# A decode step of attention and MLP on one core: eight neighbouring result rows, a second accumulator bank near the end, and re-cut weight loads

## The chip, the cores and the metric

The kernel runs on one core of a Trainium2 chip. The metric is device time in microseconds. Before the change three runs gave 212.78, 212.80 and 212.83 us, a median of 212.8. The core has these engines: TensorE (PE in the profile) multiplies matrices, VectorE (DVE) and ScalarE (ACT) do elementwise work, GpSimd (POOL) does a little at the start, and SyncE (SP) issues almost all transfers. Sixteen DMA engines move the data between device memory and the core's working memory (SBUF). Matmul results go to PSUM[...].

## What is computed

Four tokens (batch 4, one position each) of width 576 go through a layer that adds three terms:

```python
x = A_x                                    # [4, 1, 576]
xn = _layernorm(x)
out = x + A(xn) + B(xn)

# A: attention over a window of the cache
W = 2048                                   # the last 2048 of 8192 positions
q = xn @ wq                                # 32 heads of 128; 16 key/value heads
p = softmax((q . k_window) * 128 ** -0.5)
A = (p @ v_window) @ wo                    # wo: [4096, 576]

# B: an MLP; with one position the shifted first half of it gives zero
x1 = xn
B = x1 + gelu(layernorm(x1) @ w3) @ w4     # w3: [576, 4608], w4: [4608, 576]
```

In the reference B's first half pads and shifts along the sequence. With a sequence of one, every shifted part is zero, so w1 and w2 are not read. What has to be read is 87.17 MB: keys and values of the window (16 + 16 loads of 2 MB), wq and wo (4.7 MB each), w3 and w4 (5.3 MB each).

## The kernel before

The program's order is written out by hand, so that each engine executes its instructions in the order of the source. SyncE issues the loads in this order: wq, then K and V by head, with a quarter of wo ahead of every fourth V, w3 after the V of head 2, and w4 after the last V. K and V share six buffers, and a load is issued when a buffer comes free. Each load is one instruction for all 128 partitions; the transfers that one queue was given are done in order.

**Weight tiles.** D is 576 = 4 x 128 + 64. The first 512 rows of wq and of w3 are laid out with four neighbouring rows in one partition, so that one partition of the "main" part is 4 rows of wq in one run of 32 KB (w3: 36 KB). Before, this main part comes in two loads (lines 119 to 121 for wq, `load_w3` at 129 to 133), each with half of every partition's run. The last 64 rows come in a third load, spread over 128 partitions. `load_w4` brings w4's 36 row groups ("rows" below: each is 128 x 576) in pieces, cut at the points of `W4_PIECES`.

**The main loop** goes over the 16 key/value heads. For head t: VectorE transposes K (`k_transpose`), TensorE forms the scores (`k_scores`), the softmax of head t-1 and the value product (`pv`) of head t-2 run in the gaps, and the outputs of head t-3 are transposed and summed (`o_turn`, `o_sum`). After every fourth head `o_spread`, `o_pick` and `o_proj` bring the attention result into shape (the tile `op`) and multiply it with a quarter of wo. In the turn of head 7 the MLP's first product and gelu run (`mlp_g`, `mlp_turn`, `mlp_act`), whose result is the tile `gT`.

**The accumulator.** Everything that ends in the result is added up in one PSUM bank, `acc`: the layernormed x plus x (`idz`), the output projection, and the MLP's second product (`mlp_out`). The stationary operand has 32 columns, in which the four batch values stand in columns 0, 8, 16 and 24 (step `RS` = 8) with zeros between. `acc_matmuls` does two matmuls for each weight row: result columns 0 to 287 into partitions 0 to 31, columns 288 to 575 into partitions 32 to 63. So two neighbouring matmuls always stand in different groups of 32 partitions.

**The end.** After the loop come the last two heads, then w4's pieces in the order of arrival, with the last quarter of `o_proj` between the second and the third. Then VectorE casts 64 x 288 values (line 601), and SyncE stores the rows 0, 8, 16, ... of the 64 with a three-dimensional pattern (line 602).

Of the kernel before, what the change touches and what calls it, by code (L numbers as in the profile page):

```python
# [8 lines left out]
ACT = mybir.ActivationFunctionType  # L9
ALU = mybir.AluOpType  # L10
AX = mybir.AxisListType
BF16 = mybir.dt.bfloat16
F32 = mybir.dt.float32
# [9 lines left out]
def kernel(  # L23
# [14 lines left out]
    nc = tc.nc  # L38
    P = 128
    B, Sq, D = A_x.shape  # L40
# [4 lines left out]
    F = B_w3.shape[1]  # L45
    assert Sq == 1 and Dh == P and rep == 2 and B == 4 and D == 576
    KJ = 4
    NQ = Hq * Dh
    NF = F // P
    NFH = NF // 2  # L50
# [3 lines left out]
    QD = 32  # L54
# [3 lines left out]
    CW = D // 2  # L58
# [8 lines left out]
    o2 = out.flatten_outer_dims()  # L67
# [14 lines left out]
    const = ctx.enter_context(tc.tile_pool(name="const", bufs=1))  # L82
# [4 lines left out]
    ps_acc = ctx.enter_context(tc.tile_pool(name="ps_acc", bufs=1, space=PSUM))  # L87
# [3 lines left out]
    wo_tiles = {}  # L91
    kv_tiles = {}
    WOH = 8
    WOR = WOH
    WOD = P // WOH
    WOQ = WOH // rep
# [12 lines left out]
    def part(n, parts=P):  # L109
        lo = cut["at"]  # L110
        cut["at"] = lo + n
        assert cut["at"] <= WOR * D
        return first[0:parts, lo:lo + n]
# [2 lines left out]
    nc.scalar.dma_start(out=x_bf[:], in_=x2)  # L116
    wq_sb = wp.tile([P, KJ * NQ + NQ // 2], BF16, tag="w", name="wq_sb")
    wq_main = A_wq[0:KJ * P, :].rearrange("(p j) n -> p (j n)", j=KJ)
    for e in range(2):
        lo, hi = e * 2 * NQ, (e + 1) * 2 * NQ  # L120
        nc.sync.dma_start(out=wq_sb[:, lo:hi], in_=wq_main[:, lo:hi])
    nc.sync.dma_start(out=wq_sb[:, KJ * NQ:], in_=A_wq[KJ * P:D, :].rearrange("r (e f) -> (r e) f", e=2))

    def load_wo(p):
# [3 lines left out]

    def load_w3():
        t = wp.tile([P, KJ * F + F // 2], BF16, tag="w", name="w3_sb")  # L130
        src = B_w3[0:KJ * P, :].rearrange("(p j) f -> p (j f)", j=KJ)
        for e in range(2):
            nc.sync.dma_start(out=t[:, e * 2 * F:(e + 1) * 2 * F], in_=src[:, e * 2 * F:(e + 1) * 2 * F])
        nc.sync.dma_start(out=t[:, KJ * F:], in_=B_w3[KJ * P:D, :].rearrange("r (e f) -> (r e) f", e=2))
        w_tiles["w3"] = t

    W4_PIECES = [0, 10, NFH, NFH + 10, NFH + 14, NF]

    def load_w4():
        t = wp.tile([P, NF, D], BF16, tag="w", name="w4_sb")  # L140
        for lo, hi in zip(W4_PIECES, W4_PIECES[1:]):
            e = lo // NFH
# [8 lines left out]
    ident_f = ident_w[:, 0:P]  # L151
# [7 lines left out]
    def cleared(shape, name):  # L159
        t = const.tile(shape, BF16, name=name)  # L160
        flat = t[:] if len(shape) == 2 else t[:].rearrange("p a b -> p (a b)")
        flat = flat.bitcast(F32)
        nc.scalar.activation(out=flat, in_=zero[:].bitcast(F32).to_broadcast(list(flat.shape)), func=ACT.Copy)
        return t
# [2 lines left out]
    ln2T = cleared([P, KJ + 2, QD], "ln2T")  # L167
    ZP = (NSL - 1) * NJ
    qz = cleared([P, ZP + Hkv * 4 * P], "qz")
    gT = cleared([P, NF, QD], "gT")  # L170
    op = cleared([P, WOR, QD], "op")

    RS = QD // B
    acc = ps_acc.tile([P, CW], F32)
    nc.vector.memset(acc[:], 0.0)


    def layernorm(dst_f, dst_bf, src):
        st = small.tile([B, 2, nc.vector.BN_STATS_DIM], F32, tag="ln_st")
        nc.vector.bn_stats(out=st[:, 0, :], in_=src[:, 0:D // 2])  # L180
        nc.vector.bn_stats(out=st[:, 1, :], in_=src[:, D // 2:D])
        mv = small.tile([B, nc.vector.BN_AGGR_DIM], F32, tag="ln_mv")
        nc.vector.bn_aggr(out=mv[:], in_=st[:].rearrange("p a s -> p (a s)"))
        rstd = small.tile([B, 1], F32, tag="ln_rstd")
        nc.vector.tensor_scalar_add(out=rstd[:], in0=mv[:, 1:2], scalar1=eps)
        nc.gpsimd.tensor_tensor(out=rstd[:], in0=rstd[:], in1=neg_half[:], op=ALU.pow)
        nc.vector.tensor_scalar(out=dst_bf[:], in0=src[:], scalar1=mv[:, 0:1], scalar2=rstd[:, 0:1],
                                op0=ALU.subtract, op1=ALU.mult)
        if dst_f is not None:
            nc.vector.tensor_scalar(out=dst_f[:], in0=src[:], scalar1=mv[:, 0:1], scalar2=rstd[:, 0:1],  # L190
                                    op0=ALU.subtract, op1=ALU.mult)
# [28 lines left out]
    for kb in range(NQD):  # L220
        nc.vector.tensor_copy(out=sel[:, :, :, kb, :],
                              in_=ident_bf[:].rearrange("p (ib i e) -> p ib e i", ib=2, e=2))
# [19 lines left out]
    with nc.allow_low_precision("zeros and ones"):  # L242
# [7 lines left out]
                          in_=sel_j[:].unsqueeze(1).to_broadcast([P, NG, NJ]))  # L250
# [5 lines left out]
    own = const.tile([P, WOH], F32)  # L256
    nc.vector.reduce_sum(out=own[:], in_=ident_f[:].rearrange("p (h d) -> p h d", h=WOH), axis=AX.X)

    idz = const.tile([B, QD], F32)
    nc.gpsimd.memset(idz[:], 0.0)  # L260
    nc.gpsimd.tensor_copy(out=idz[:, 0:QD:RS], in_=ident_f[0:B, 0:B])
    xsum = xn_f
    nc.vector.tensor_tensor(out=xsum[:], in0=xn_f[:], in1=x_bf[:], op=ALU.add)
    for i in range(2):
        nc.tensor.matmul(out=acc[i * QD:(i + 1) * QD, :], lhsT=idz[:], rhs=xsum[:, i * CW:(i + 1) * CW],
                         start=False, stop=False, skip_group_check=True)
    ln2_bf = part(D, B)
    layernorm(None, ln2_bf, xn_bf)
    transposed(ln2_bf, ln2T)
# [24 lines left out]
    for r in range(2):  # L294
        nc.vector.tensor_copy(out=q_bf[:, r],
                              in_=qT_ps[:, r].rearrange("p u (g x) -> p g u x", g=NQD)[:, :, :, 0:B])
    qs_ps = ps_m.tile([P, Hkv, 4, rep, B], F32, tag="m", name="qs_ps")
    for ie in range(4):
        ib, e = divmod(ie, 2)
        nc.tensor.matmul(out=qs_ps[:, :, ie], lhsT=sel[:, ib, e].rearrange("p k i -> p (k i)"),  # L300
                         rhs=q_bf.rearrange("p r g u b -> p (r g u b)"), start=True, stop=True)
    for kb in range(NQD):
        rows = slice(kb * QD, (kb + 1) * QD)
        dst = qz[rows, ZP:].rearrange("p (x m) -> p x m", m=P)[:, :, kb * QD:kb * QD + NJ].rearrange("p x (b r) -> p x b r", r=rep)
        src = qs_ps[rows].rearrange("p h i r b -> p (h i) b r")
# [2 lines left out]
        else:  # L308
            nc.vector.tensor_copy(out=dst, in_=src)  # L309


    def acc_matmuls(lhsT, rhs):
        for i in range(2):
            nc.tensor.matmul(out=acc[i * QD:(i + 1) * QD, :], lhsT=lhsT, rhs=rhs[:, i * CW:(i + 1) * CW],  # L314
                             start=False, stop=False, skip_group_check=True)

    S_ps = {}
    E = {}
# [77 lines left out]
    def o_turn(h):  # L396
        oT = ps_m.tile([P, NSL, P], F32, tag="m", name="oT")
        o = O_sb.pop(h)
        for s in range(NSL):
            nc.tensor.transpose(out=oT[:, s, :], in_=o[:, s, :], identity=ident_w[:, s * NJ:s * NJ + P])  # L400
        st["oT", h] = oT

    def o_sum(h):
        oT = st.pop(("oT", h))
        v = oT[:].rearrange("p s (g x) -> p (s g) x", g=NQD)[:, :, 0:NJ].rearrange("p g (b r) -> p b r g", r=rep)
        k = h % WOQ
        if k == 0:
            st["on"] = small.tile([P, WOH, B], BF16, tag="on", name="on")
        with nc.allow_low_precision("summed in float32"):
            nc.vector.reduce_sum(out=st["on"][:, k * rep:(k + 1) * rep, :].rearrange("p r b -> p b r"),  # L410
                                 in_=v, axis=AX.X)
# [12 lines left out]
    def o_pick(h):  # L424
        if h % WOQ < WOQ - 1:
            return
        R = st.pop("R")
        mk = small.tile([P, WOR, WOH, B], BF16, tag="mk")
        nc.vector.tensor_tensor(out=mk[:], in0=R[:],
                                in1=own[:].unsqueeze(1).unsqueeze(3).to_broadcast([P, WOR, WOH, B]), op=ALU.mult)  # L430
        with nc.allow_low_precision("one term is not zero"):
            nc.vector.reduce_sum(out=op[:, :, 0:QD:RS], in_=mk[:].rearrange("p i h b -> p i b h"), axis=AX.X)

    def o_proj(h):
        if h % WOQ < WOQ - 1:
            return
        for i in range(WOR):
            acc_matmuls(op[:, i, :], wo_tiles[h // WOQ][:, i, :])

    G_CHUNKS = [(e, 4 * g, 4) for e in range(2) for g in range(NQD)] + [(e, 16, 2) for e in range(2)]  # L440
    xs = const.tile([P, NF, B], F32, name="g_x")
# [31 lines left out]
    def mlp_act():  # L473
        u = const.tile([P, NF, B], F32, name="g_u")
        nc.vector.tensor_tensor(out=u[:], in0=xs[:], in1=xs[:], op=ALU.mult)
        nc.vector.tensor_scalar(out=u[:], in0=u[:], scalar1=GELU_A, scalar2=1.0, op0=ALU.mult, op1=ALU.add)
        nc.vector.tensor_tensor(out=u[:], in0=u[:], in1=xs[:], op=ALU.mult)
        nc.scalar.activation(out=u[:], in_=u[:], func=ACT.Tanh, scale=GELU_C)
        nc.vector.tensor_scalar(out=u[:], in0=u[:], scalar1=0.5, scalar2=0.5, op0=ALU.mult, op1=ALU.add)
        nc.vector.tensor_tensor(out=gT[:, :, 0:QD:RS], in0=u[:], in1=xs[:], op=ALU.mult)  # L480

    def mlp_out(lo, hi):
        w4 = w_tiles["w4"]
        for i in range(lo, hi):
            acc_matmuls(gT[:, i, :], w4[:, i, :])


    order = [("K", 0), ("K", 1), ("K", 2)]
# [24 lines left out]
    for t in range(Hkv):  # L513
        hm, hv, hf, hp = t - 1, t - 2, t - 3, t - 4
        for s in range(NSL):
            if s == NSL - 1 and hm >= 0:
                sm_turn(hm)
            n = t * NSL + s + 1
# [68 lines left out]
    o_turn(hl - 1)  # L587
    o_sum(hl - 1)
    pieces = list(zip(W4_PIECES, W4_PIECES[1:]))
    mlp_out(*pieces[0])  # L590
    o_turn(hl)
    o_sum(hl)
# [1 line left out]
    o_pick(hl)  # L594
    mlp_out(*pieces[1])
    o_proj(hl)
    for lo, hi in pieces[2:]:
        mlp_out(lo, hi)

    fin = const.tile([2 * QD, CW], out.dtype)  # L600
    nc.vector.tensor_copy(out=fin[:], in_=acc[0:2 * QD, :])
    nc.sync.dma_start(out=o2.rearrange("b (i n) -> i b n", i=2), in_=fin[0:2 * QD:RS, :])


# [28 lines left out]
```

## Time and profile before

| | us |
|---|---|
| median of three runs | 212.8 |
| profiled execution, span | 211.0 |
| TensorE busy | 150.4 (71%) |
| VectorE busy | 121.3 (57%) |
| ScalarE busy | 33.9 (16%) |
| load queue (q1), packets' time as a share of 16 engines' span | 97.2% |
| HBM read | 87.17 MB, 413 GB/s over the span |

The span is measured from the first to the last instruction of one profiled execution; the run's time has 1.8 us more around it. The page shows busy time by engine, a line for the DMA engines in forty slices of the span, and a chain of work followed back from the last instruction. By line that chain puts 29% of the span on the loads of w3 and w4, 26% on V, and 12% on K; by engine 67% on DMA and 18% on TensorE. In the timeline a row gives start, length, engine, source line, operation, output and inputs, and how many instructions are merged; in brackets is the idle time ahead of it, and what ended it. SPq is SyncE's queue: the length there is the time of issuing, and the data comes later. For a group of merged matmuls the length is that of the whole group.

### The profile page before, as it was taken

The numbers are of one execution on the slowest core, as the hardware profiler recorded it, in microseconds if no ns is written. First come the engines' busy times: TensorE is split into PE (matmuls) and PEld (weight loads), VectorE is DVE, ScalarE is ACT, GpSimd is POOL, SyncE is SP. The second block draws the span as 40 slices with busy tenths as digits, with TensorE's granted clock in tenths as the row PEclk, the third lists the DMA queues.
The fourth block names the chain that finished last, engine by engine and source line by source line (L and its number), as shares of the span: only waits on it lengthen the run. The fifth ranks groups of instructions, "written<-read, shape, count | busy, mean of one in ns | idle before, by whom it ended". The sixth has DMA issues, their size and how long they took to land.

```text
span 211.0 us, 2402 instructions
## 1 busy us (share of the span) xinstructions
PE 150.4 (71%) x955; PEld 62.2 (29%) x955; DVE 121.3 (57%) x216; ACT 33.9 (16%) x63; POOL 2.8 (1%) x15
## 2 busy tenths in 40 slices
PE   0386695869395009669999499968693967898982
PEld 0122232224132003214454144334240322433561
DVE  4832989485731082825725968985867284763220
ACT  7703101021102000202121121120211020202300
POOL 4010000000000000000000000000000000000000
PEclk9999579799859655957999669999998596969998
DMA  7999999999999999999999999999999999999990
GB/s 246 435 413 441 422 441 410 443 435 413 450 419 426 438 419 429 434 444 432 416 438 435 416 427 437 435 432 424 436 426 426 420 444 435 422 429 429 425 382 30
DMA packets 6797, 87.32 MB, mean 414 GB/s; under 512 B 758, under 2 KB 770, under 8 KB 1282
## 3 DMA queue, kind: packets, MB, share of 16 engines
q1 hardware_dynamic: 6778, 87.17, 97.2%
q8 instruction: 7, 0.11, 0.2%
q14 instruction: 4, 0.03, 0.0%
q10 hardware_dynamic: 8, 0.00, 0.0%
HBM read 87.17 MB, written 0.00 MB: 413 GB/s over the span
## 4 chain that ended last, share of the span: by engine, by line
DMA 67%; PE 18%; DVE 7%; issue 4%; ACT 1%; SPq 1%; POOL 0%; POOLq 0%; DVEq 0%
DMA w_sb<-in_B_w_dram 29%; DMA vn<-in_A_v_cache_dram 26%; DMA kn<-in_A_k_cache_dram 12%; PE S L335 9%; DVE kt L215 3%; PE g_ps L453 2%; PE q_ps L277 2%; PE O L387 2%; PE oT L400 1%; PE acc L314 1%; DMA first<-in_A_x_dram 1%; DVE qz L309 1%; PE gT_ps L465 1%; DVE mx L341 1%; PE S L357 1%
## 5 line engine op out<-in xcount | busy, mean ns | idle before, releaser
L335 PE MATMUL S<-kt,qz 128*128 128x512 bf16 x256 | 82.0, 452 | 3.1 <-DVE kt L215 3.1
L215 DVE STREAM_TRANSPOSE kt<-kn 128x1024 int32<-128x1024 int32 x64 | 76.8, 1221 | 10.3 <-DMA kn<-in_A_k_cache_dram 9.4
L387 PE MATMUL O<-vn,PT 128*32 128x512 bf16 x256 | 27.8, 434 | 38.5 <-DMA vn<-in_A_v_cache_dram 36.9
L335 PEld LDWEIGHTS <-qz 128*128 128x128 bf16 x256 | 22.2, 106 | 43.2 <-issue 28.5
L363 ACT ACTIVATE E<-S 128x512 bf16<-128x512 f32 x16 | 9.5, 597 | 123.4 <-PE S L357 123.4
L387 PEld LDWEIGHTS <-PT 128*32 128x32 bf16 x256 | 7.3, 95 | 47.2 <-DVE kt L215 23.8
L369 DVE STREAM_TRANSPOSE PT<-E 128x512 bf16<-128x512 bf16 x16 | 11.4, 711 | 14.3 <-ACT E L363 14.3
L353 DVE TENSOR_REDUCE nm<-mg 8x1 bf16<-8x16 f32 x16 | 2.5, 154 | 20.3 <-PE mg L348 20.2
L394 ACT ACTIVATE O_sb<-O,rd 128x512 f32<-128x512 f32 x16 | 11.0, 687 | 16.5 <-issue 11.0
L410 DVE TENSOR_REDUCE on<-oT 128x8 bf16<-128x128 f32 x16 | 4.6, 286 | 15.7 <-PE oT L400 15.7
L400 PE MATMUL oT<-ident_w,O_sb 128*128 128x128 f32 x64 | 11.8, 315 | 0.0
L341 DVE TENSOR_REDUCE mx<-S 128x1 f32<-128x512 f32 x16 | 10.5, 658 | 1.3 <-PE S L335 1.3
L400 PEld LDWEIGHTS oT<-ident_w,O_sb 128*128 128x128 f32 x64 | 9.6, 167 | 5.4 <-issue 3.9
L357 PE MATMUL S<-nm,j_row 8*128 8x512 bf16 x16 | 6.9, 431 | 0.0
L373 PEld LDWEIGHTS dn<-rs,same_j 128*128 128x128 f32 x32 | 5.8, 188 | 2.9 <-ACT E L363 0.7
L326 PE MATMUL S<-negbig,ohT 4*128 4x512 bf16 x16 | 6.2, 385 | 0.0
L314 PE MATMUL acc<-w_sb,gT 128*32 128x288 bf16 x72 | 5.3, 287 | 1.2 <-DMA w_sb<-in_B_w_dram 1.2
L348 PE MATMUL mg<-dm,sel_jb 128*8 128x16 bf16 x16 | 2.8, 175 | 3.7 <-DVE dm L343 3.7
L348 PEld LDWEIGHTS <-sel_jb 128*8 128x8 bf16 x16 | 1.3, 83 | 12.6 <-issue 6.7
L453 PE MATMUL g_ps<-w_sb,ln2T 128*32 128x512 bf16 (+1 forms) x50 | 4.9, 443 | 0.0
L314 PE MATMUL acc<-wo_sb,op 128*32 128x288 bf16 x64 | 4.6, 287 | 0.0
L373 PE MATMUL dn<-rs,same_j 128*128 128x1 f32 x32 | 4.6, 212 | 0.0
(89 smaller groups left out, 72.8 us busy)
## 6 DMA issues: line engine op xcount, KB each, us to landing
kn<-in_A_k_cache_dram SPq DMA_DIRECT2D x16, 2048.0 KB, 22.3
vn<-in_A_v_cache_dram SPq DMA_DIRECT2D x16, 2048.0 KB, 23.9
wo_sb<-in_A_wo_dram SPq DMA_DIRECT2D x4, 1152.0 KB, 25.8
w_sb<-in_B_w_dram SPq DMA_DIRECT2D x2, 2304.0 KB, 31.4
wq_sb<-in_A_wq_dram SPq DMA_DIRECT2D x2, 2048.0 KB, 9.6
w_sb<-in_B_w_dram SPq DMA_DIRECT2D x2, 1440.0 KB, 29.2
w_sb<-in_B_w_dram SPq DMA_DIRECT2D x3, 576.0 KB, 30.5
w_sb<-in_B_w_dram SPq DMA_DIRECT2D x1, 1152.0 KB, 28.7
```

Source lines behind the costliest of these rows:

```text
L215: nc.vector.transpose(out=kt[:], in_=src)
L314: nc.tensor.matmul(out=acc[i * QD:(i + 1) * QD, :], lhsT=lhsT, rhs=rhs[:, i * CW:(i + 1) * CW], start=False, stop=False, skip_group_check= ...
L335: nc.tensor.matmul(out=S_ps[h][:], lhsT=qz[:, z0:z0 + P], rhs=kt[:, ib, :, e:2 * QD:2].rearrange("p c k -> p (c k)"), start=False, stop=Fa ...
L341: nc.vector.reduce_max(out=mx[:], in_=S_ps[h][:], axis=AX.X)
L357: nc.tensor.matmul(out=S_ps[h][:], lhsT=j_row[:], rhs=st.pop(("nm", h))[:, 0:1].to_broadcast([NJ, NW]), start=False, stop=False, skip_grou ...
L363: nc.scalar.activation(out=E[h][:].rearrange("p c k -> p (c k)"), in_=S_ps.pop(h)[:], func=ACT.Exp, scale=scale, accum_out=rs[:])
L369: nc.vector.transpose(out=PT[h][:], in_=E.pop(h)[:])
L373: nc.tensor.matmul(out=dn[:], lhsT=same_j[:], rhs=st.pop(("rs", h))[:], start=True, stop=True)
L387: nc.tensor.matmul(out=O_ps[h][g * QD:(g + 1) * QD], lhsT=PT[h][:, c, :], rhs=vn[:, :, c, :], start=(s == 0), stop=False, skip_group_check ...
L394: nc.scalar.activation(out=O_sb[h][:], in_=O_ps.pop(h)[:], func=ACT.Copy, scale=st.pop(("rd", h))[:, 0:1])
L400: nc.tensor.transpose(out=oT[:, s, :], in_=o[:, s, :], identity=ident_w[:, s * NJ:s * NJ + P])
L453: nc.tensor.matmul(out=g_ps[g * QD:(g + 1) * QD], lhsT=ln2T[:, k, :], rhs=rhs, start=(j == 0), stop=False, skip_group_check=True)
```

## The change

Five edits:

- The main part of wq comes in one load in place of two; so does the main part of w3.
- w4's last piece of four rows is cut into two of two rows (seven cut points, six loads).
- The stationary tiles `gT`, `op` and `idz` have 10 columns in place of 32. The batch values stand in columns 1, 3, 5 and 7, with zeros around them. `acc_matmuls` takes 8 of the 10 columns: from column 1 for the first half of the result, from column 0 for the second. So the values of batch b land in row 2b for the first half and in row 2b + 1 for the second, both in rows 0 to 7 of the accumulator. Only zeros are added to the other rows.
- `acc_matmuls` takes a list of terms. After the last values (from the first w4 piece on) there is a second bank, `acc_odd`, and odd terms go to its partitions 32 to 39. This lasts through the last `o_proj` and w4's first four pieces (rows 0 to 31). Then ScalarE copies the eight rows of `acc_odd` to SBUF, and the last two pieces go to `acc` alone.
- In place of the cast VectorE adds `acc` and the copy (8 x 288), and the store is of eight whole rows to neighbouring places.

```diff
-    for e in range(2):
-        lo, hi = e * 2 * NQ, (e + 1) * 2 * NQ
-        nc.sync.dma_start(out=wq_sb[:, lo:hi], in_=wq_main[:, lo:hi])
+    nc.sync.dma_start(out=wq_sb[:, 0:KJ * NQ], in_=wq_main)
...
-        src = B_w3[0:KJ * P, :].rearrange("(p j) f -> p (j f)", j=KJ)
-        for e in range(2):
-            nc.sync.dma_start(out=t[:, e * 2 * F:(e + 1) * 2 * F], in_=src[:, e * 2 * F:(e + 1) * 2 * F])
+        nc.sync.dma_start(out=t[:, 0:KJ * F], in_=B_w3[0:KJ * P, :].rearrange("(p j) f -> p (j f)", j=KJ))
...
-    W4_PIECES = [0, 10, NFH, NFH + 10, NFH + 14, NF]
+    W4_PIECES = [0, 10, NFH, NFH + 10, NFH + 14, NF - 2, NF]
...
-    gT = cleared([P, NF, QD], "gT")
-    op = cleared([P, WOR, QD], "op")
-
-    RS = QD // B
+    OR = 2 * B
+    OW = OR + 2
+    gT = cleared([P, NF, OW], "gT")
+    op = cleared([P, WOR, OW], "op")
+
...
+    second = []
+
+    def acc_matmuls(terms):
+        for i in range(2):
+            for n, (lhsT, rhs) in enumerate(terms):
+                to, q, start = (second[0], QD, second[1]) if second and n % 2 else (acc, 0, False)
+                nc.tensor.matmul(out=to[q:q + OR, :], lhsT=lhsT[:, 1 - i:1 - i + OR],
+                                 rhs=rhs[:, i * CW:(i + 1) * CW], start=start, stop=False, skip_group_check=True)
+                if start:
+                    second[1] = False
...
-    def acc_matmuls(lhsT, rhs):
-        for i in range(2):
-            nc.tensor.matmul(out=acc[i * QD:(i + 1) * QD, :], lhsT=lhsT, rhs=rhs[:, i * CW:(i + 1) * CW],
-                             start=False, stop=False, skip_group_check=True)
...
-        for i in range(WOR):
-            acc_matmuls(op[:, i, :], wo_tiles[h // WOQ][:, i, :])
+        for i in range(0, WOR, 2):
+            acc_matmuls([(op[:, i + u, :], wo_tiles[h // WOQ][:, i + u, :]) for u in range(2)])
...
-        for i in range(lo, hi):
-            acc_matmuls(gT[:, i, :], w4[:, i, :])
+        for i in range(lo, hi, 2):
+            acc_matmuls([(gT[:, i + u, :], w4[:, i + u, :]) for u in range(2)])
...
+    acc_odd = ps_acc.tile([P, CW], F32, tag="g", name="acc_odd")
+    second += [acc_odd, True]
     mlp_out(*pieces[0])
...
-    for lo, hi in pieces[2:]:
+    mlp_out(*pieces[2])
+    mlp_out(*pieces[3])
+    second.clear()
+    odd = const.tile([OR, CW], F32)
+    nc.scalar.activation(out=odd[:], in_=acc_odd[QD:QD + OR, :], func=ACT.Copy)
+    for lo, hi in pieces[4:]:
         mlp_out(lo, hi)
 
-    fin = const.tile([2 * QD, CW], out.dtype)
-    nc.vector.tensor_copy(out=fin[:], in_=acc[0:2 * QD, :])
-    nc.sync.dma_start(out=o2.rearrange("b (i n) -> i b n", i=2), in_=fin[0:2 * QD:RS, :])
+    fin = const.tile([OR, CW], out.dtype)
+    nc.vector.tensor_tensor(out=fin[:], in0=acc[0:OR, :], in1=odd[:], op=ALU.add)
+    nc.sync.dma_start(out=o2.rearrange("b (i n) -> (b i) n", i=2), in_=fin[:])
```

Left out above: the values are written with step 2 from column 1 (`op`, `gT`, `idz`), and the first use of the accumulator, for x, goes through `acc_matmuls` too.

More of the change, by code (lines that the diff above doesn't have):

```diff
@@ L257 @@
     nc.vector.reduce_sum(out=own[:], in_=ident_f[:].rearrange("p (h d) -> p h d", h=WOH), axis=AX.X)
-    idz = const.tile([B, QD], F32)
+    idz = const.tile([B, OW], F32)
     nc.gpsimd.memset(idz[:], 0.0)
-    nc.gpsimd.tensor_copy(out=idz[:, 0:QD:RS], in_=ident_f[0:B, 0:B])
+    nc.gpsimd.tensor_copy(out=idz[:, 1:OR + 1:2], in_=ident_f[0:B, 0:B])
     xsum = xn_f
     nc.vector.tensor_tensor(out=xsum[:], in0=xn_f[:], in1=x_bf[:], op=ALU.add)
-    for i in range(2):
-        nc.tensor.matmul(out=acc[i * QD:(i + 1) * QD, :], lhsT=idz[:], rhs=xsum[:, i * CW:(i + 1) * CW],
-                         start=False, stop=False, skip_group_check=True)
+    acc_matmuls([(idz[:], xsum)])
     ln2_bf = part(D, B)
@@ L309 @@
             nc.vector.tensor_copy(out=dst, in_=src)
-    def acc_matmuls(lhsT, rhs):
-        for i in range(2):
-            nc.tensor.matmul(out=acc[i * QD:(i + 1) * QD, :], lhsT=lhsT, rhs=rhs[:, i * CW:(i + 1) * CW],
-                             start=False, stop=False, skip_group_check=True)
     S_ps = {}
@@ L431, in o_pick @@
         with nc.allow_low_precision("one term is not zero"):
-            nc.vector.reduce_sum(out=op[:, :, 0:QD:RS], in_=mk[:].rearrange("p i h b -> p i b h"), axis=AX.X)
+            nc.vector.reduce_sum(out=op[:, :, 1:OR + 1:2], in_=mk[:].rearrange("p i h b -> p i b h"), axis=AX.X)
     def o_proj(h):
@@ L479, in mlp_act @@
         nc.vector.tensor_scalar(out=u[:], in0=u[:], scalar1=0.5, scalar2=0.5, op0=ALU.mult, op1=ALU.add)
-        nc.vector.tensor_tensor(out=gT[:, :, 0:QD:RS], in0=u[:], in1=xs[:], op=ALU.mult)
+        nc.vector.tensor_tensor(out=gT[:, :, 1:OR + 1:2], in0=u[:], in1=xs[:], op=ALU.mult)
     def mlp_out(lo, hi):
         w4 = w_tiles["w4"]
-        for i in range(lo, hi):
-            acc_matmuls(gT[:, i, :], w4[:, i, :])
+        for i in range(lo, hi, 2):
+            acc_matmuls([(gT[:, i + u, :], w4[:, i + u, :]) for u in range(2)])
     order = [("K", 0), ("K", 1), ("K", 2)]
```

## The prediction

> **What bounds the kernel now.** I read the page's forty slices first, then the chain that ended last, then SyncE's own timeline, then the last 16 us. From the page:
>
> ```profile
> DMA  7999999999999999999999999999999999999990
> GB/s 246 435 413 441 422 441 410 443 435 413 450 419 426 438 419 429 434 444 432 416 438 435 416 427 437 435 432 424 436 426 426 420 444 435 422 429 429 425 382 30
> ...
> q1 hardware_dynamic: 6778, 87.17, 97.2%
> ```
>
> The 16 DMA engines are full from the second slice to the last but one: 97.2% of 211.0 us is 205.1 us per engine, which is the time between the first load's start (about 1.6 us) and the last one's end (about 206.5). So the span is: start about 1.6 us, 205 us of stream, and a tail. Compute matters only where it starves the queue or stands behind the last byte. SyncE's timeline shows how far ahead the queue is:
>
> ```profile
> 13.00 0.54 SPq L102 DMA_DIRECT2D vn<-in_A_v_cache_dram  x1
> ...
> 171.43 8.94 SPq L144 DMA_DIRECT2D w_sb<-in_B_w_dram  x5
> 208.21 0.68 SPq L602 DMA_DIRECT2D out_dram<-fin  x1
> ```
>
> The last w4 load is issued at about 180 us and lands at 207.0; a K or V load takes 22 to 24 us from issue to landing (part 6 of the page). A delay of a few us in compute is therefore invisible. The issue at 13.00 waited for the second half of wq, so that half landed then. Now the tail, in the timeline of the end:
>
> ```profile
> 202.64 1.16 PE L314 MATMUL acc<-wo_sb,op 128*32 128x288 bf16 x16
> 203.51 0.10 PEld L314 LDWEIGHTS <-gT 128*32 128x32 bf16 x1
> 204.27 2.04 PE L314 MATMUL acc<-w_sb,gT 128*32 128x288 bf16 x28 [0.47 <-DMA w_sb<-in_B_w_dram]
> ...
> 207.03 0.67 PE L314 MATMUL acc<-w_sb,gT 128*32 128x288 bf16 x8 [0.72 <-DMA w_sb<-in_B_w_dram]
> ...
> 207.73 0.45 DVE L601 CAST fin<-acc 64x288 bf16<-64x288 f32 x1 [5.14 <-PE acc L314]
> 208.21 0.68 SPq L602 DMA_DIRECT2D out_dram<-fin  x1
> ```
>
> PE is idle for 0.72 us, then gets the last four w4 rows: 8 matmuls 0.67, cast 0.45, issue of the store 0.68, then 211.0 - 208.89 = 2.1 us of store and closing. These 4 us are what the change can touch, beside the stream itself. And the DMA slices of 205 to 211 us (0.15 us each):
>
> ```profile
> DMA  3664555342000000000000000000000000100000
> GB/s 154 277 276 184 215 246 215 154 184 92 0 0 0 0 0 0 0 0 0 0 0 0 0 0 0 0 0 0 0 4 27 0 0 0 55 0 0 0 0 0
> ```
>
> Two things: for the last 1.5 us only about half of the engines still move data, so the last piece waits for the late half; and the store's packets (slices 30 and 31) start about 209.35, 0.45 us after its issue ended.
>
> **What the Trainium skill says.** "TensorE: Matmul & The Clock Gate", Part 3: matmuls whose outputs stand in different 32-partition groups run concurrently. The trace agrees: 16 matmuls of 286 ns each take 1.16 us, one new start each (1.16 - 0.286)/15 = 58 ns, half of the 120 ns that 288 columns take at the rate of L335 (four 512-column matmuls in 1.01 us, starts 208 to 213 ns apart, full clock). "DMA: Bandwidth & Descriptors", "Why a DMA increments its semaphore by 16 and not by 1": a DMA is spread over the largest number of engines up to 16 that divides the slowest dimension on both sides. The trace's packet records agree for the store: 2x4x288 gives two completion writes, so two engines with four 576-byte packets each. By this 8x288 goes to eight engines, one packet each. "PSUM — Partial Sum Buffer", "The four PSUM rules": a first matmul clears the accumulate bits of its whole bank in the quadrants that it writes, so one start for the new bank is enough; no run here shows it yet.
>
> **Part by part.**
>
> *wq and w3 in one load.* Each DMA engine carries 8 of the 128 rows. In the packet records a 16,384-byte packet takes 611 ns and a 4,608-byte one 178: 36.8 ns per 1,000 bytes and 9 ns a packet, and a completion write 9. (Starts are 607 and 174 apart, so the real cost is 5 to 9 ns.) wq and w3 save 8 packets and one completion per engine each; the w4 piece split in two adds 8 and one. Net 9 small items: 0.04 to 0.08 us, taken as -0.06. Nothing in the trace shows a packet of 32 or 36 KB; 18,432 bytes take 686, on the same line. Bounds: the first packets of all engines took about 1.2 us against 0.611, and half a dozen second ones 250 to 520 ns extra; if one long packet pays this once, up to -0.3; if long packets disturb, +0.1. What waits: the first q matmul started at 12.90 when wq's first half had long landed, held by the layernorm work ahead of it; now it needs all of wq's main part, at 12.95. That is under 0.1 us on a chain that feeds a queue 20 us ahead: nothing. SyncE issues one instruction fewer at each place (0.4 us); the later loads move forward by that and land no earlier, as the stream is full.
>
> *8 result rows, narrower weights.* gT and op shrink (clears of 0.66 and 0.29 us on ACT, both off the path), weight loads have 8 columns. Both halves now accumulate in rows 0 to 7, one column group. In the loop o_proj has no second bank: 16 matmuls at 120 ns, 15 x 0.12 + 0.286 = 2.09 instead of 1.16 us, three times, with scores queued behind. Hidden by the 22 us lead of the loads; without that cover 2.8 us. From the last values on, odd weight rows go to the second bank in the next column group, so pieces 0 to 3 and the last o_proj alternate groups as before: same rate, PE still waits for the w4 data.
>
> *Seventh cut point of w4: the last four rows as two and two.* In the records the last pieces land 1.40 us apart (204.2, 205.6, 207.0); now 205.6, 206.3, 207.0. PE ends rows 28 to 31 at 206.31 as before. Rows 32 and 33: four serial matmuls, started 206.31, issued by 206.8, still ahead of the last arrival. Rows 34 and 35: 3 x 0.12 + 0.286 = 0.65 instead of 0.67. So halving the rows gains -0.02, because the pairing over two groups is gone here.
>
> *ACT copy of the second bank.* Needs the last odd matmul (206.3) and takes about 0.45 (8x288; DVE's cast of that length took 0.45): done near 206.8, 0.9 us before it is needed. It stands on ACT alone with nothing behind. Without cover +0.45.
>
> *The final add.* A two-input op over 256 float32 columns took 0.43 (mk, L429), i.e. 0.16 + 256 x 1.04 ns; with 288 columns 0.46 against the cast's 0.45: +0.01.
>
> *The store.* Issue 0.68 now. Bounds: 0.33, the fastest two-dimensional loads when issued alone (L126), and 0.68, no change. Three-dimensional K loads take 0.54 each time, x (4x576) 0.56. I take 0.42, the median of the w4 loads: -0.26, range -0.35 to 0. Data starts 0.45 after the issue ends, so all of it counts. Then one packet for four in a row: 3 x 29 ns, -0.09.
>
> *Sum*, against the profiled execution: -0.06 - 0.02 + 0.01 - 0.26 - 0.09 = -0.42. Its span is 211.0, the median outside 212.8, 1.8 us around the span that no part touches. 212.8 - 0.42 = 212.38, say 212.4.
>
> **Rivals.**
>
> - *The store's issue stays at 0.68* (it is the price of a small store, not of its dimensions). For it: x, small and flat, took 0.56. Against: K at 0.54 and flat loads at 0.33 differ by shape. Then 212.8 - 0.16 = 212.65.
> - *The stream itself shortens more*: the long first packets pay the start once, -0.3, and the store is as fast as 0.33: 212.8 - 0.42 - 0.3 = 212.1, and a little less with both, 212.0.
> - *Slower: serial accumulation into one column group doesn't hide its weight loads.* Before, no two neighbouring acc matmuls used the same group. If each takes its 287 ns and then a load of 95, four take 1.53 us: rows 32 and 33 end at 206.31 + 1.53 = 207.84, the last rows at 209.37 instead of 207.70, +1.67, with the other items (-0.40): 214.1. It decides from a spacing of about 0.28 us on, where it adds 0.8 (two groups of four, 206.31 + 8 x 0.28 = 208.55). Against it: L335 runs same-place matmuls with full 128-column loads of 106 ns at full rate.
> - *The ACT copy isn't hidden*, a false wait for instance, +0.45: 212.8, no change. Against: its bank has no later writer.
> - The diff does make what it says (six w4 loads, from seven cut points); that part can't fail.
>
> **How the numbers follow.** Forecast 212.4: 0.50, with its own range 212.2 to 212.6. Issue unchanged or copy not hidden: 0.20. Stream shorter: 0.20. Slower: 0.10, into which I also put an engine of the late half being delayed twice. The range 211.95 to 212.8 leaves out the slow case and half of the short-stream one. 0.2% is 0.43 us, about what a measurement of this kernel can tell from no change: the bound is 212.37, almost on the forecast. Faster: 0.30 of the forecast's half and nearly all of the short stream, 0.49; within: 0.41; slower: 0.10.
>
> **What would show it.** The store's issue (0.42) and its engines; the last four matmuls in about 0.65 and starting near 207.0; the copy over before the final add; first q matmul near 13.0; DMA still full in all middle slices; 128 packets fewer on q1 and two-row packets at the end. Wrong if the last matmuls start before 206.6 or after 207.3 (then the stream changed), or if their spacing is far from 0.12.

## The result, and the profile after

The changed kernel takes 212.2 us (median of five runs, 212.08 to 212.34) against 212.8 (five runs, 212.67 to 212.97). The ratio is 0.9974, with a 95% interval of 0.9961 to 0.9986: faster by 0.26%. A second measurement of the same kernel, beside later experiments, gave 212.29 against 212.72, a ratio of 0.9979 (0.9970 to 0.9988). The profiled execution's span went from 211.0 to 210.4 us.

First the page of the changed kernel: the slices of the DMA engines, and the load queue with its packets, megabytes and share.

```profile
DMA  7999999999999999999999999999999999999991
...
q1 hardware_dynamic: 6640, 87.17, 97.4%
...
kn<-in_A_k_cache_dram SPq DMA_DIRECT2D x16, 2048.0 KB, 22.2
```

The load queue is as full as before, with 138 packets fewer (6778 to 6640), and a K load still waits 22 us in the queue. So the loads fill the middle of the kernel as they did before. Now the timeline of the end: start, length, engine, line, operation.

```profile
206.35 0.40 ACT L604 ACTIVATE odd<-acc_odd 8x288 f32<-8x288 f32 x1 [7.80 <-PE acc_odd L181]
206.39 1.35 PE L181 MATMUL acc<-w_sb,gT 128*8 128x288 bf16 x8
...
207.09 0.33 PEld L181 LDWEIGHTS <-gT 128*8 128x8 bf16 x3 [0.25 <-issue]
207.85 0.45 DVE L609 TENSOR_TENSOR fin<-acc,odd 8x288 bf16<-8x288 f32 x1 [5.95 <-PE acc L181]
208.32 0.37 SPq L610 DMA_DIRECT2D out_dram<-fin  x1
```

The eight matmuls are rows 32 to 35. The second four start with the weight loads (`LDWEIGHTS`) at 207.09, when the last piece has landed. Before, the last matmuls started at 207.03, the cast at 207.73 and the store's issue at 208.21. So up to the store the changed kernel is *later*, by 0.11 us. The whole gain comes after that point. The DMA slices of 205 to 211 us (0.15 us each) show the store's packets:

```profile
DMA  6555455532100000000000000001000001000000
GB/s 277 200 200 215 184 215 215 200 154 92 77 0 0 0 0 0 0 0 0 0 0 0 0 0 0 0 0 31 0 0 0 0 0 55 0 0 0 0 0 0
```

They stand in slice 27, at about 209.1; before, they started at 209.49 in the packet records. Step by step, with the packet and semaphore records of the two traces:

| step, us | before | after | difference |
|---|---|---|---|
| last w4 piece there, matmuls start | 207.03 | 207.09 | +0.06 |
| last matmuls (8 paired, 4 serial) | 0.67 | 0.65 | -0.02 |
| last matmul's end to VectorE's start | 0.04 | 0.11 | +0.07 |
| cast, add | 0.45 | 0.45 | 0.00 |
| the store's issue | 0.68 | 0.37 | -0.31 |
| issue's end to first packet | 0.60 | 0.42 | -0.18 |
| first packet to landing | 0.49 | 0.46 | -0.03 |
| landing to the end of the span | 0.99 | 0.85 | -0.14 |
| sum | | | -0.54 |

That is the difference of the spans (210.97 to 210.43). The rounding of single rows leaves 0.01. "Landing" is the moment of the last semaphore increment of a transfer. The stretch of the last row, from the store's landing to the end of the span, is called the closing below.

### The profile page after: what moved, and what is told of

Same layout as the page of the kernel before. It is cut to its first block, busy times and chain, and to the rows that moved or that the text cites. A ratio compares the mean times of both kernels' runs of the same rounds, so it can differ in the third digit from the quotient of the medians.

```text
span 210.4 us, 2389 instructions
## 1 busy us (share of the span) xinstructions
PE 149.7 (71%) x941; PEld 63.7 (30%) x955; DVE 120.3 (57%) x216; ACT 33.9 (16%) x64; POOL 2.8 (1%) x15
## 3 DMA queue, kind: packets, MB, share of 16 engines
q1 hardware_dynamic: 6640, 87.17, 97.4%
## 4 chain that ended last, share of the span: by engine, by line
DMA 69%; PE 19%; DVE 8%; issue 1%; ACT 1%; SPq 0%; DVEq 0%
DMA vn<-in_A_v_cache_dram 37%; DMA w_sb<-in_B_w_dram 27%; PE S L336 7%; DMA wq_sb<-in_A_wq_dram 6%; DVE kt L223 4%; PE acc L181 2%; PE g_ps L454 2%; PE O L388 2%; PE q_ps L283 2%; PE oT L401 1%; DVE mx L342 1%; PE S L358 1%; DVE qz L315 1%; PE gT_ps L466 1%; PE qT_ps L298 0%
## 5 line engine op out<-in xcount | busy, mean ns | idle before, releaser
L336 PE MATMUL S<-kt,qz 128*128 128x512 bf16 x242 | 76.8, 440 | 5.0 <-DVE kt L223 3.1
L388 PE MATMUL O<-vn,PT 128*32 128x512 bf16 x256 | 27.2, 424 | 37.7 <-DMA vn<-in_A_v_cache_dram 32.5
L181 PE MATMUL acc<-wo_sb,op 128*8 128x288 bf16 x56 | 7.7, 290 | 0.0
L181 PE MATMUL acc<-w_sb,gT 128*8 128x288 bf16 x40 | 5.9, 285 | 1.3 <-DMA w_sb<-in_B_w_dram 1.2
L181 PEld LDWEIGHTS <-op 128*8 128x8 bf16 x64 | 4.6, 88 | 2.6 <-issue 0.7
L472 DVE COPY g_x<-gT_ps 128x64 f32<-128x64 f32 (+1 forms) x3 | 0.6, 194 | 7.7 <-PE gT_ps L466 7.7
```

The source lines that it names most:

```text
L181: nc.tensor.matmul(out=to[q:q + OR, :], lhsT=lhsT[:, 1 - i:1 - i + OR], rhs=rhs[:, i * CW:(i + 1) * CW], start=start, stop=False, skip_gro ...
L336: nc.tensor.matmul(out=S_ps[h][:], lhsT=qz[:, z0:z0 + P], rhs=kt[:, ib, :, e:2 * QD:2].rearrange("p c k -> p (c k)"), start=False, stop=Fa ...
L388: nc.tensor.matmul(out=O_ps[h][g * QD:(g + 1) * QD], lhsT=PT[h][:, c, :], rhs=vn[:, :, c, :], start=(s == 0), stop=False, skip_group_check ...
```

## The experiments

The theory to test was that the gain is the store's form, with nothing from the loads, and that the second bank only pays for the narrower accumulation. All runs below were timed beside the kernel before (212.72 to 212.75 in these sessions). The changed kernel is 212.2 to 212.3.

### The old form of the store

The eight rows are put in another order (first halves in rows 0 to 3, second halves in rows 4 to 7), so that the store's pattern is the old one. All else stays changed.

```diff
-    OW = OR + 2
+    OW = OR + B
...
-    lhsT=lhsT[:, 1 - i:1 - i + OR]
+    lhsT=lhsT[:, (1 - i) * B:(1 - i) * B + OR]
...
-    nc.sync.dma_start(out=o2.rearrange("b (i n) -> (b i) n", i=2), in_=fin[:])
+    nc.sync.dma_start(out=o2.rearrange("b (i n) -> i b n", i=2), in_=fin[:])
```

> The changed kernel with one part taken back: the eight rows stand as first halves (0 to 3) and second halves (4 to 7), so the store has the old three-dimensional pattern (2x4x288), all else as changed. Theory (the gain is the store's form): issue of the store back from 0.37 to about 0.68 us, first data 0.60 in place of 0.42 after the issue's end, eight packets on two engines; about 0.5 to 0.6 us longer than the changed kernel, 212.75, no different from the kernel before. Rival (the gain is in the loads or the accumulation): it stays at 212.2 to 212.3 with an issue near 0.4.

Measured: 212.78 us (13 runs), a ratio to the kernel before of 1.0001 (0.9993 to 1.0009). The gain is gone. The timeline of SyncE's queue at the end of this kernel:

```profile
208.40 0.79 SPq L610 DMA_DIRECT2D out_dram<-fin  x1
```

The issue takes 0.79 us, and the first packet comes 0.60 after it, as in the kernel before. The issue is 0.11 longer than the 0.68 of the kernel before, which had been expected here; the runs don't show why. In the changed kernel the form of the store alone is worth about 0.5 us, as much as the whole change brought. That doesn't mean that the other parts do nothing: the run with the new loads in the kernel before shows below that two of them cancel.

### Dimensions or engines

The old store has three dimensions and goes to two DMA engines; the new one has two dimensions and goes to eight. To separate these, each of the eight rows gets a gap in its middle, so that the store is three-dimensional and stays on eight engines.

```diff
-    fin = const.tile([OR, CW], out.dtype)
+    fin = const.tile([OR, 2, CW // 2 + 16], out.dtype)
...
-    nc.sync.dma_start(out=o2.rearrange("b (i n) -> (b i) n", i=2), in_=fin[:])
+    nc.sync.dma_start(out=o2.rearrange("b (i u n) -> (b i) u n", i=2, u=2), in_=fin[:, :, 0:CW // 2])
```

> The changed kernel with a gap inside each of the eight rows of the stored tile, so that the store is three-dimensional (two runs of 288 bytes a row) but still goes to eight engines. Theory A (the slow store comes from its dimensions): issue 0.54 to 0.7 us, first data 0.6 after it, 212.6 to 212.75. Theory B (it comes from going to two engines): issue 0.37, data 0.42 after it, 0.04 more for the second run: 212.3. Theory C (both have a part): issue from dimensions, the wait after it from engines, 212.45.

Measured: 212.87 us (21 runs), ratio 1.0006 (1.0000 to 1.0013). SyncE's row at the end of the timeline:

```profile
208.22 0.88 SPq L611 DMA_DIRECT2D out_dram<-fin  x1
```

Theory A's cause holds, and C's split does not: the wait after the issue is 0.60 although eight engines are used. The issue (0.88) and the time are both above theory A's ranges (0.54 to 0.7, and 212.6 to 212.75). Over all twelve traces the wait from the issue's end to the first packet is 0.597 to 0.599 us in the four with a three-dimensional store and 0.419 to 0.440 in the eight with a two-dimensional one. So both costs go with the third dimension. One thing is not separated: this run also cuts the rows into runs of 288 bytes, where the other stores have 576. And the length of the issue doesn't follow from the dimensions alone: the four three-dimensional stores took 0.67, 0.68, 0.79 and 0.88 us, the K loads, three-dimensional too, mostly 0.54. The number of engines hardly shows: from the first packet to the landing it took 0.46 to 0.49 us on two engines and 0.45 to 0.47 on eight. The number of engines itself is as the Trainium skill has it ("DMA: Bandwidth & Descriptors", "Why a DMA increments its semaphore by 16 and not by 1"): the changed store has eight completion writes (4-byte packets, one for each engine) in the packet records, the old one two.

### The loads of wq and w3 in halves

```diff
-    nc.sync.dma_start(out=wq_sb[:, 0:KJ * NQ], in_=wq_main)
+    for e in range(2):
+        lo, hi = e * 2 * NQ, (e + 1) * 2 * NQ
+        nc.sync.dma_start(out=wq_sb[:, lo:hi], in_=wq_main[:, lo:hi])
```

(and the same for w3)

> The changed kernel with the main parts of wq and w3 in two loads each again. Theory (the loads' cut is worth next to nothing, one engine's 16 packets and two completion writes less, 0.08 to 0.16 us of packet overhead at most): 212.2 to 212.35, stream of 204.9 to 205.1 us. Rival 1 (long first packets cost start-up time: they took 1.9 us against 1.23 for later ones): faster by 0.1, 212.1. Rival 2 (the long loads carry the gain): 212.6 or more.

Measured: 212.35 us (19 runs), ratio 0.9981 (0.9975 to 0.9988). That is 0.06 to 0.15 above the changed kernel. In its trace the stream (first load packet to the end of the last one) takes 205.05 us. The changed kernel has 204.97, and 205.40 in the second profile; the kernel before has 204.91. So the scatter of the stream from run to run is larger than any effect of the cut. The closing is 0.97 us against 0.85, which is enough for all of the difference in the medians (see below). Rival 2 falls; rival 1 is not seen.

### Without the second bank

Everything is summed in one bank, and so in one group of 32 partitions; the copy is left out, and a cast stands in place of the final add.

```diff
-    acc_odd = ps_acc.tile([P, CW], F32, tag="g", name="acc_odd")
-    second += [acc_odd, True]
...
-    second.clear()
-    odd = const.tile([OR, CW], F32)
-    nc.scalar.activation(out=odd[:], in_=acc_odd[QD:QD + OR, :], func=ACT.Copy)
...
-    nc.vector.tensor_tensor(out=fin[:], in0=acc[0:OR, :], in1=odd[:], op=ALU.add)
+    nc.vector.tensor_copy(out=fin[:], in_=acc[0:OR, :])
```

> The changed kernel without the second bank, so without the copy, and with a cast in place of the final add. Theory (matmuls into one column group start 0.1215 us apart, so the end becomes bound by TensorE): from the landing at 204.27, 40 + 16 matmuls less those that wait: rows 18 to 27 issued by 206.7, 28 to 31 by 207.67, 32 and 33 by 208.16, the last ends near 208.8 instead of 207.74: +1.0 us, 213.2. Rival (TensorE waits for w4 anyway, the second bank pays for nothing): 212.2, the last matmuls still begin at 207.1.

Measured: 215.82 us (6 runs), ratio 1.0144 (1.0121 to 1.0167): the second bank is worth far more than I expected. TensorE's timeline in this kernel:

```profile
199.63 2.62 PE L181 MATMUL acc<-w_sb,gT 128*8 128x288 bf16 x20
202.17 0.66 PE L401 MATMUL oT<-ident_w,O_sb 128*128 128x128 f32 x4
203.21 0.35 PE L420 MATMUL R<-on,sel_wo 128*128 128x32 bf16 x8 [0.38 <-DVE on L411]
203.49 2.12 PE L181 MATMUL acc<-w_sb,gT 128*8 128x288 bf16 x16
205.45 2.12 PE L181 MATMUL acc<-wo_sb,op 128*8 128x288 bf16 x16
207.41 4.57 PE L181 MATMUL acc<-w_sb,gT 128*8 128x288 bf16 x36
```

My expectation counted only the rows that wait for the last loads. But rows 0 to 17 and the last output projection are serial too. From 203.49 on TensorE no longer waits for any load: 68 matmuls at 0.122 us fill the time to 212. In this execution it was also 1.35 us behind in the last loop turn already (the projection of the third quarter starts at 189.39 instead of 188.04). The six runs fall into two groups, 215.1 to 215.3 and 216.4 to 216.6; the profiled one is of the upper group. If this delay is what separates them, taking the 1.35 away from the profiled 214.6 leaves 213.2, which is 2.8 above the changed kernel's span; the lower group of times is 2.9 above its time. Such a delay is not this kernel's own: in the profile of the kernel before the same projection starts at 189.68, and in the one with wq and w3 in halves the first w4 matmuls start at 199.52 instead of 198.27. There TensorE later waits for w4 anyway, and the delay is covered. Where it comes from is open.

The run takes away two things at once, the second bank and the second group of 32 partitions. The kernel before paired its matmuls over two groups of one bank (58 ns apart, in the prediction). So what is shown is the worth of the pairing; that a bank of its own is needed for it is not shown.

### The last four rows of w4 in one piece

```diff
-    W4_PIECES = [0, 10, NFH, NFH + 10, NFH + 14, NF - 2, NF]
+    W4_PIECES = [0, 10, NFH, NFH + 10, NFH + 14, NF]
```

> The changed kernel with w4's last four rows in one piece again. Theory (all that follows the last landing is serial): 8 matmuls into one column group, 7 x 0.1215 + 0.286 = 1.14 in place of 0.65 us after the landing: +0.49, 212.7. Rival (the last landing comes earlier with fewer packets, or the matmuls are paired in some other way): within 0.1 of 212.2.

Measured: 213.16 us (16 runs), ratio 1.0020 (1.0013 to 1.0027): 0.9 above the changed kernel, nearly twice what was expected. The end of its timeline:

```profile
206.86 1.14 PE L181 MATMUL acc<-w_sb,gT 128*8 128x288 bf16 x8 [0.70 <-DMA w_sb<-in_B_w_dram]
...
208.11 0.45 DVE L609 TENSOR_TENSOR fin<-acc,odd 8x288 bf16<-8x288 f32 x1 [6.42 <-PE acc L181]
208.58 0.36 SPq L610 DMA_DIRECT2D out_dram<-fin  x1
```

The matmuls take the 1.14 us that were expected. The rest comes after the store: from its landing to the end of the span this kernel needs 1.36 us, where the changed kernel needs 0.85. The kernel has one transfer fewer than the changed one. So the next run keeps the piece of four rows, and the number of transfers too, by loading w4's first piece in two.

```diff
+        cuts = [0, 4] + W4_PIECES[1:]
-        for lo, hi in zip(W4_PIECES, W4_PIECES[1:]):
+        for lo, hi in zip(cuts, cuts[1:]):
```

> The changed kernel with w4's last four rows in one piece, but with its first piece loaded in two (4 and 6 rows), so that SyncE issues as many loads as in the changed kernel. Theory (the last piece costs only its matmuls, and the rest of e4's 0.96 us came from SyncE's closing, 1.36 in place of 0.85 us, which depends on how many transfers the program has): closing 0.85 again, +0.49 for the matmuls, 212.7. Rival (the larger last piece itself makes the closing long): 213.1 as e4.

Measured: 212.63 us (13 runs), ratio 1.0000 (0.9992 to 1.0008), and a closing of 0.84. Beside it, the changed kernel once more:

> The changed kernel once more, as it is, beside the next ones on the same chip. All theories: 212.2, and a closing stretch (from the store's landing to the end of the span) of 0.85 us.

Measured: 212.29 us (12 runs), closing 0.85; its profiled execution was the longest, 212.65, and its last load packets ended at 207.17 instead of 206.73. So the piece of four costs 0.34 to 0.43 us in these medians and 0.49 in the trace, and the closing follows the number of transfers. All traces together, by the number of transfers that SyncE issues. At the end of the program SyncE makes five waits in a row for semaphores; the table says which of them is the wait for the store, and where a gap of 0.43 to 0.46 us stands in this row:

| transfers | closing, us | the store's wait | the gap is ahead of | kernels |
|---|---|---|---|---|
| 46 | 1.36 | fourth | the fifth wait | last four rows in one piece |
| 47 | 0.84 to 0.85 | fifth | the fourth | changed (twice), and six experiments |
| 48 | 0.99 | third | the third | before |
| 48 | 0.90 | fourth | the third | two pieces of one row |
| 49 | 0.97 | third | the second | wq and w3 in halves |

This reading explains the closings. The transfers use eight semaphores in turn, so their number decides which wait is the store's. With 47 transfers it is the last of the five, and the closing is shortest. One wait behind it makes 0.90, two make 0.97 to 0.99; that is the 0.14 us between the kernel before and the changed one. The gap stands one wait earlier with each transfer more. With 47 and more it is over before the store lands; with 46 it comes after, and 0.90 + 0.45 = 1.35 us. What SyncE does in the gap is open: the record shows no work there.

### The new loads in the kernel before

```diff
-    for e in range(2):
-        lo, hi = e * 2 * NQ, (e + 1) * 2 * NQ
-        nc.sync.dma_start(out=wq_sb[:, lo:hi], in_=wq_main[:, lo:hi])
+    nc.sync.dma_start(out=wq_sb[:, 0:KJ * NQ], in_=wq_main)
...
-    W4_PIECES = [0, 10, NFH, NFH + 10, NFH + 14, NF]
+    W4_PIECES = [0, 10, NFH, NFH + 10, NFH + 14, NF - 2, NF]
```

(w3 likewise; accumulation, cast and store are those of the kernel before)

> The kernel before with the loads of the changed one alone (wq and w3 in one load each, w4's last four rows as two and two); accumulation, cast and store stay as they were. Theory: its last two rows are four paired matmuls, 0.13 + 0.286 = 0.42 in place of 0.67, -0.25, and the closing goes from 0.99 to 0.85, -0.14; the store stays slow: 212.75 - 0.39 = 212.36. Rival (the loads give nothing without the store): 212.75.

Measured: 212.50 us (21 runs), ratio 0.9990 (0.9983 to 0.9996). The direction is as expected, with 0.22 of the 0.39 us. So the loads do gain something without the store. In the profiled execution (212.32, one of the shorter ones) both terms are there: the closing is 0.85, and the end of the timeline shows the paired matmuls:

```profile
206.96 0.42 PE L310 MATMUL acc<-w_sb,gT 128*32 128x288 bf16 x4 [0.27 <-DMA w_sb<-in_B_w_dram]
206.96 0.11 PEld L310 LDWEIGHTS <-gT 128*32 128x32 bf16 x3 [0.48 <-issue]
207.42 0.45 DVE L597 CAST fin<-acc 64x288 bf16<-64x288 f32 x1 [5.81 <-PE acc L310]
207.89 0.67 SPq L598 DMA_DIRECT2D out_dram<-fin  x1
```

Four paired matmuls take 0.42 us, where the changed kernel needs 0.65 for four serial ones. What stands against these gains in the other runs of this kernel is not settled; one trace can't tell.

Set beside the run with the old form of the store, this one prices the new accumulator. Both have the new loads, 47 transfers and a three-dimensional store; they differ in the narrow rows, the second bank and the add, and the one that has them takes 212.78 instead of 212.50 us. So the accumulator costs 0.25 to 0.3 us. The larger parts in the traces are four serial matmuls (0.65 for 0.42), a longer issue of the store (0.79 for 0.67) and the later start of the add (0.07). The change as a whole is then, by these medians, about -0.2 from the loads, +0.25 from the accumulator, and -0.5 from the store that the accumulator makes possible.

### A shorter last piece

After the last landing only the last piece's matmuls count. So the last two rows are loaded one by one.

```diff
-    W4_PIECES = [0, 10, NFH, NFH + 10, NFH + 14, NF - 2, NF]
+    W4_PIECES = [0, 10, NFH, NFH + 10, NFH + 14, NF - 2, NF - 1, NF]
```

(with an odd number of rows a piece ends in a single term)

> The changed kernel with w4's last piece of two rows cut into one and one (seven loads). Theory: two matmuls after the last landing, 0.1215 + 0.286 = 0.41 in place of 0.65, so -0.24; one transfer more gives the closing stretch of the kernel before, 0.97 to 0.99 in place of 0.85, +0.13: 212.1. Rival (the closing depends on the store's form alone): 211.95. Rival (a landing is late for small pieces): 212.3 or more.

Measured: 212.01 us (6 runs), ratio 0.9967 (0.9954 to 0.9979). In its trace the last matmul ends 0.25 us earlier than in the changed kernel, and the closing is 0.90. A second form loads w4's first 18 rows in one piece, so that the number of transfers is again 47, and turns and sums the last head ahead of them:

> The changed kernel with w4's last two rows in pieces of one and one, and w4's first 18 rows in one load (so as many transfers as in the changed kernel); the last head's turn, sum and spread go ahead of these rows. Theory: two matmuls after the last landing (0.41 in place of 0.65), closing 0.85: 212.0, the fastest of all. Rival (the matmuls of rows 0 to 17 now start only at their landing near 200.8 and run into the next pieces): 212.2 or more.

Measured: 211.93 us (5 runs, 211.91 to 212.01), ratio 0.9963 (0.9951 to 0.9976). It has the lowest median of all; from the form with seven loads (212.01, 211.84 to 212.20) it can't be told apart. The end of its timeline:

```profile
206.33 1.14 PE L182 MATMUL acc<-w_sb,gT 128*8 128x288 bf16 x8
...
207.57 0.45 DVE L610 TENSOR_TENSOR fin<-acc,odd 8x288 bf16<-8x288 f32 x1 [6.73 <-PE acc L182]
208.05 0.37 SPq L611 DMA_DIRECT2D out_dram<-fin  x1
```

The eight matmuls of rows 32 to 35 now run without a gap from 206.33 to 207.47, and the last piece landed at 207.01, just ahead of the first matmul that needs it (207.06). So TensorE, and no longer the last landing, sets the end here.

## Why the prediction was right, and where its terms were off

The forecast of 212.4 us stands beside 212.2 measured. The second measurement has 212.29 against 212.72, a gain of 0.43 where 0.42 was forecast. The direction, the place (after the last landing, mostly the store) and the range hold. By its own steps:

- **The store's issue**: -0.26 predicted, -0.31 measured (0.68 to 0.37). Taking two-dimensional loads as the nearest row was right, and the rival that a small store costs 0.68 in any form falls with the 0.37 of the changed kernel.
- **The store after its issue**: this is the term that was mis-sized. The prediction took the 0.45 us to the first packet as fixed and gave -0.09 for the packets. In the records it was 0.60 and became 0.42, and to the landing there is another -0.03: -0.20 together. The 0.45 was read from the edge of a slice of 0.15 us (209.35; the first packet starts at 209.49); and it was not known that a third dimension also delays the first packet. The packets' -0.09 was too large.
- **The closing**: not in the sum at all ("no part touches" what is around; but this stretch lies inside the span), -0.14. It belongs to the number of transfers, by the table above: with the new loads SyncE issues 47 in place of 48. The prediction gives no reason for this gain, so it is luck.
- **The stream**: -0.06 predicted. The last matmuls start 0.06 later in the profile, and the stream scatters by some tenths between executions, so that neither sign can be told. 138 packets fewer don't show. (Before, the stream ran from 1.74 to 206.66 us in the records, where the prediction took about 1.6 and 206.5.) The first packets of 32 KB took 0.2 to 1.0 us more than later ones, the first ones of 16 KB before took 0.3 to 1.1 us more, so nothing is saved at the start. (Three of the second packets took 250 to 520 ns extra before, not half a dozen.) The rival of a shorter stream falls.
- **Narrow rows in one column group**: the serial spacing is 0.1215 us where 0.12 was assumed; the slower rival (weight loads not hidden) falls. The basis was misread: the starts of the score matmuls (L335) are 224 ns and more apart in the records, not 208 to 213 ns. The 1.01 us stands in the chain, where the piece begins at 101.68, 0.07 after the start of the first of the four matmuls. At the usual 226 ns, 288 columns would have given 127 ns, so that 0.12 came out so near is luck. The last four take 0.65 as predicted, and the projection in the loop 2.12 for 2.09, covered by the loads. That the pairing goes on in the second bank at the old rate held too; without it the kernel takes about 2.9 us more.
- **ScalarE's copy**: done at 206.75, 1.1 us before it is needed. The rival of an uncovered copy falls.
- **wq in one load**: the first q matmul started at 13.09 us instead of 12.90, where under 0.1 was predicted; it is hidden all the same.
- **The final add**: +0.01 predicted; its own time is right (0.45), but it starts 0.11 us after the last matmul, where the cast starts 0.04 after it. In the run without a second bank, where the same eight rows are only cast, it is 0.04 again. So the add costs 0.07 more through its start. The chain of the changed kernel shows an instruction of VectorE's sequencer ahead of the add:

```profile
207.78 0.02 DVEq L609
```

It is a wait for TensorE; the add itself waits for ScalarE's copy. A product that has one operand in PSUM and one in SBUF too, but a single wait, starts 0.04 after its last matmul's end (200.98) in the same trace:

```profile
200.63 0.35 PE L420 MATMUL R<-on,sel_wo 128*128 128x32 bf16 x8 [0.38 <-DVE on L411]
201.02 0.42 DVE L430 TENSOR_TENSOR mk<-R,own 128x256 bf16<-128x256 f32 x1 [0.44 <-PE R L420]
```

So the later start goes with the second wait, and not with the place of the operands.

The errors have different signs: the store and the closing gave 0.30 us more than predicted (0.65 for 0.35), the stream and the add took about 0.18. So the forecast was nearer to the result than its terms, and that is luck.

## What to carry to other kernels

Where the transfers fill the whole kernel, as here, the time that this change could reach is behind the last landing, and each step there counts in full: the number of matmuls in the last piece, the start of the last vector operation, and the form of the store. Lay the result out in PSUM so that one two-dimensional store writes neighbouring rows; here that was worth 0.5 us, and the accumulator that it needs took about half of it back. If narrower accumulation takes the pairing of two groups of 32 partitions away, put every second term into another group (here in a second bank), and look at the whole serial backlog, not only at the matmuls that wait for data. And where a step of 0.1 us counts, look at which wait of the closing is the store's: one transfer fewer cost 0.5 us here.

## What was not expected of the hardware

- A three-dimensional store costs twice: 0.67 to 0.88 us of issue in place of 0.36 to 0.37, and 0.60 in place of 0.42 to 0.44 us from there to the first packet, on two engines or on eight.
- The closing was 0.84 to 0.85 us in eight traces with 47 transfers, 0.90 to 0.99 with 48 and 49, and 1.36 with 46. It depends on how many of SyncE's waits stand behind the store's, and on whether the gap of 0.43 to 0.46 us among them comes before or after the landing.
- The final add, which waits for TensorE and for ScalarE, started 0.107 to 0.108 us after its last matmul in nine traces; the final cast, with one wait, 0.037 after it in three. In all twelve traces three other copies and casts from PSUM with two waits started 0.105 to 0.113 us after theirs, and a product of one operand in PSUM and one in SBUF, with one wait, 0.036 to 0.038.
